# First batch's head: where four projection halves and the next chunk's rows are loaded, how many preparation ticks stand ahead of stage 3, and one half on the short form

## The chip, the cores and the metric

The kernel runs on one core of one Trainium2 chip. The metric is the device time of one execution in microseconds; lower is better. PE is TensorE, DVE is VectorE, ACT is ScalarE, POOL is GpSimd; SP is the engine that only issues transfers. POOL and ACT issue some transfers too.

## The reference

Two blocks in a row. The first mixes along the sequence with a filter in the frequency domain, the second is a SwiGLU feed-forward block on the result:

```python
X = np.fft.rfft(x, axis=1)                      # x: (8, 3008, 256)
Y = X * (filt_r + 1j * filt_i)[None]            # 1505 frequencies
y = np.fft.irfft(Y, n=3008, axis=1)
t = y.reshape(8 * 3008, 256)
g, val = t @ w_gate, t @ w_val                  # (256, 1536) each, float64 in memory
out = (g / (1 + np.exp(-g)) * val) @ w_out      # (1536, 256)
```

The weights arrive as 64-bit floats. The engines compute in 32 bits, so the kernel itself turns each weight into a 32-bit float, out of the two 32-bit words of the 64-bit number.

## The kernel before

**Batches, chunks, groups.** The eight batches are worked through in turn. For each, the transform over 3008 = 47 x 64 is made of matrix products in stages. `stage1` is the transform over 47, `stage2a` that over 64 with the filter, `stage2b` goes back over 64, `stage3` back over 47. `stage3` is done for one chunk of the sequence at a time (four chunks) and leaves the chunk's transposed tokens in `y`. The feed-forward part takes each chunk with three groups of hidden blocks, so a batch has 12 steps. In the first batch the order of the first nine steps is groups outside, chunks 0 to 2 inside, so steps 0, 1 and 2 all use group 0. A step's instructions stand in a list written out by hand (`SCHEDULE`): `P`, `Q`, `A`, `B`, `E` are products on PE (`product`, L1070; profile names `wk`, `wa`, `we`), the lower-case letters evictions on DVE and ACT, `D` and `S` sums on POOL, `W` and `o` the output projection (L1167). Fewer multiplications are bought by sums: `combine_sequence` makes sums of the parts of `y` in `y_t` (mostly on POOL), on which the `A`, `B`, `E` products run.

**The order on an engine is the order in the program.** Every instruction is pinned (`pin`), and each engine takes its own in that order. A transfer's issue stands in the queue of the engine that issues it; most are on SP.

**The head.** Before step 0 the whole spectral part of the first batch has to run, in the scope that opens with `spool0`. `stage2a`, a sum on POOL and `stage2b` are staggered over units `u` of 2 of the 24 frequencies, `stage2b` four units behind. Each `stage2b` (L935) leaves its unit in one of four buffers, and SP stores it to the DRAM tensor `d` (`d2` in the code; L952), from where the rows of a chunk are read back in another order (`load_rows`, L676). The units from 10 on (`N_STORED = 10`) have their share of chunk 0 copied straight into the buffer `f0` (L940); their stores to `d` are put off, and `store_rest(nc.gpsimd)` issues them from POOL. In front of them POOL copies one column of `f0` into `one` (L1276), which holds POOL until chunk 0's rows have landed. Then SP loads chunk 1's rows (`load_t4(1, i)`, two loads of 96 partitions), which need the put-off stores. Seven `idle` products keep PE turning, and `stage3` of chunk 0 follows: four products (`wpd`, L976), each evicted into `y` by ACT (L988, L996) or DVE (L328, L1000).

**The weights.** Between these instructions a `Preparation` converts the weights. They come in halves of 256 KB in a fixed order: 0 to 7 are group 0's hidden weights, 8 to 11 the first four halves of the output projection, 12 on the hidden weights of group 1. `load_weights(i)` (L389) issues a half's load; the first 12 (`N_EARLY`) have places of their own and are loaded by hand-placed calls: 0 to 7 at the start on SP, 8 to 11 from POOL at `u` = 5 to 8. `round_half(i)` is the conversion, spread over ticks: two DVE instructions (L411, L414) with an ACT one (L416), then two DVE ones (L420, L423) for halves below `N_SHORT`, three ACT ones (L427, L429, L431) for the others, then DVE L434 and L438, then POOL (L446 for the projection, with four sums after each second half; L458, L459 for hidden weights). Half `i` < 8 begins at tick 4 `i`; halves 8, 9, 10, 11, 12 begin at ticks 44, 48, 52, 56, 60.

`preparation.tick(step, n)` emits the next `n` ticks where it stands, so its place in the program is the place of those instructions in the engines' queues. `finish(0)` in the head runs to tick 44, the following `tick(0, 5)` to tick 49. In steps 0, 1 and 2 one tick is emitted at each place of the schedule that `tick_at` lists: 18 in step 0, 20 each in steps 1 and 2. Step 3 begins on group 1's weights, in the buffer `lent`, and so needs those.

Of the kernel before, what the change touches and what calls it, by code (L numbers as in the profile page):

```python
# [54 lines left out]
NS, NQ = 24, 64  # L55
NR = 2 * N1
NK = 4 * NS

NH = 4
# [12 lines left out]
N_TWO = NS // NV  # L72
N_QUAD = 8
N_FOUR = NS // 4
N_STORED = 10
# [130 lines left out]
def kernel(  # L206
# [10 lines left out]
    nc = tc.nc  # L217
# [149 lines left out]
    def bits(a):  # L367

        t = wo_t.rearrange("p j i f -> p (j i f)")[:, a:a + 512]
        return t.bitcast(U32).rearrange("p (b f two) -> p b f two", b=2, two=2)  # L370

    def spot_of(i):

        spot = (i - N_EARLY) % 5
        return spot if i < N_LENT and spot < 3 else None

    N_EARLY = 12
    N_SHORT = 9

    def load_weights(i, queue=nc.sync):  # L380
        if i in raws or i >= len(weights):
            return
        if i < N_EARLY:
            raws[i] = early_raw(i)
        elif spot_of(i) is not None:
            raws[i] = bits(4 * 7 * 128 + 512 * spot_of(i))
        else:
            raws[i] = rpool.tile([128, 2, 128, 2], U32, name=f"raw_{i}", tag="raw", bufs=2)
        pin(queue.dma_start(out=raws[i], in_=weights[i][0]))  # L389

    def round_half(i):
# [26 lines left out]
        pf = pw.bitcast(FP32)  # L418
        if i < N_SHORT:
            pin(v.tensor_scalar(out=pf, in0=pw, scalar1=-896.0, scalar2=0.0,  # L420
# [74 lines left out]
    class Preparation:  # L495
# [3 lines left out]
        def __init__(self):  # L499
# [9 lines left out]
            for i, (_, (use, *at)) in enumerate(weights):  # L509
# [14 lines left out]
                def go(half=half, i=i):  # L524
# [3 lines left out]

                times = (0, 1, 2, 3, 4, 6, 7, 9, 10) if i >= N_SHORT else \
                    (0, 1, 2, 3, 4, 6, 9, 10)  # L530
# [33 lines left out]
        def finish(self, step):  # L564
            while any(s <= step and self.at <= t for s, t in self.need.items()):
# [1 line left out]
                self.tick(step)  # L567

    preparation = Preparation()
    tick_at = [set(range(40, 162, 7)), *[{n * 174 // 20 for n in range(20)}] * 2,  # L570
               {0, 6, 12, 18, 24, 31, 37, 42, 72, 78, 84, 90, 96, 102, 108, 114, 122, 130, 138, 146}]

    back_t, quad_t = [], []
# [14 lines left out]
    def bank(name):  # L588
        return wps.tile([128, 512], FP32, name=f"w{name}", tag="w")
# [4 lines left out]
    def idle(t, banks, n):  # L594

        for ps in banks:
            pin(nc.tensor.matmul(out=ps[:, 0:n], lhsT=t[:, 0:128], rhs=t[:, 0:n],
                                 start=True, stop=True))

    class Spectral:  # L600
# [75 lines left out]
            pin(queue.dma_start(out=t.rearrange("p (o n) c -> p o (n c)", o=1),  # L676
                                in_=self.d2_rows[k, steps, :, n].rearrange("s a n c -> s a (n c)")))

        def load_t4(self, k, i):
            t = t4pool.tile([128, NH, C], FP32, name=f"t4_{self.b}_{k}_{i}", tag="t4")  # L680
            at = 2 * k + i
            if self.b == 0:
                self.load_rows(t[0:NK], k, slice(0, NS), ts(i, NH))
            else:

                rows = self.d2_tokens.rearrange("(h n) a c -> h (n a) c", h=2)
                rows = rows[:, ts(at, 2 * NS * NH)]
                for j in range(2):
                    self.load(out=t[64 * j:64 * j + 64, 1],
                              in_=rows[j, 128 * (1 - j):128 * (1 - j) + 64])  # L690
                    self.load(out=t[:, 2 * j], in_=rows[j, 64 * j:64 * j + 128])
            self.t4[k, i] = t
# [498 lines left out]
    spec = Spectral(0)  # L1191

    def run(piece):
        for _ in piece:
            pass

    with tc.tile_pool(name="start", bufs=1) as spool0:
        x0_t = spool0.tile([128, 8, C], FP32, name="x0")
        x0.append(x0_t[0:NR])
        tb0 = spool0.tile([128, NS, 2, 128], FP32, name="tb0")  # L1200
        f0 = spool0.tile([128, NS, C], FP32, name="f0")
        room = spool0.tile([128, 9 * NV, C], FP32, name="room")
        units = [room[:, ts(i, NV)] for i in range(9)] + [x0_t[:, ts(i, NV)] for i in range(4)]
        units += [y_f[:, ts(i, NV * C)].rearrange("p (i c) -> p i c", c=C) for i in range(6)]
        early_places = {"p": (0, 5), "t2": (5, 3), "g": (9, 4), "q": (13, 3), "fr": (16, 3)}
        zero = units[8].rearrange("p i c -> p (i c)")

        one_t = lent[:, 0:2 * NK * 32].rearrange("p (b k) -> p b k", b=2)
        spare = []
        n = 0  # L1210
        while n < NPR - 1:
            pair = ORDER[n][0] in "ABE" and ORDER[n + 1][0] in "ABE"
            spare += [n] if pair else []
            n += 2 if pair else 1

        def early(tag, u):
            first, count = early_places[tag]
            return units[first + u % count]

        def early_raw(i):  # L1220
            if i >= 8:
                return bits(4 * 7 * 128 + 512 * (i - N_EARLY))
            t = wt_t[:, spare[i]:spare[i] + 2].rearrange("p s z f -> p (s z f)")
            return t.bitcast(U32).rearrange("p (b f two) -> p b f two", b=2, two=2)

        unit_t = spool0.tile([128, 128], FP32, name="unit")
        pin(nc.scalar.dma_start(out=unit_t, in_=unit_dram.ap()))
        pin(nc.vector.memset(zero, 0.0))
        pin(nc.scalar.activation(out=one, in_=off_t, func=AF.Silu))
        idle(zero, [bank("idle") for _ in range(3)], 512)  # L1230
        pin(nc.sync.dma_start(out=wf_t, in_=wf_dram.ap()))
        load = [("x", 0), ("w", 0), ("x", 1), ("w", 1), ("w", 2), ("x", 2), ("w", 3), ("w", 4),
                ("x", 3), ("w", 5), ("w", 6), ("w", 7)] + [("t", n) for n in range(6)]
        for what, i in load:
            {"x": spec.load_x, "w": load_weights, "t": spec.load_tables}[what](i)
        for u in range(8):
            idle(zero, [bank("idle") for _ in range(2 * (u in (4, 6)))], 512)
            spec.stage1_first(u)
            preparation.tick(0, (4, 2, 4, 2, 5, 3, 2, 6)[u])
        idle(zero, [bank("idle") for _ in range(2)], 512)  # L1240
        for u in range(2):
            spec.turn(u)
        idle(zero, [bank("idle") for _ in range(2)], 512)
        preparation.tick(0, 5)
        spec.real_part(0)
        lag = 4
        for u in range(N_TWO + lag):
            if u < N_TWO:
                spec.turn(u + 2)
                step = spec.stage2a(u)  # L1250
                next(step)
                if u % 3 == 1:
                    spec.real_part(u + 2)
                next(step)
                preparation.tick(0, 2 * (u < 3), hold=True)
                run(step)
                preparation.release()
                if u % 3 != 2:
                    spec.real_part(u + 1)
            if u == N_TWO + lag - 1:  # L1260
                preparation.finish(0)
            if u >= lag:
                if u == N_TWO:
                    idle(zero, [bank("idle")], 512)
                run(spec.stage2b(u - lag))
            if u == 6:
                pin(nc.sync.dma_start(out=wi_t, in_=wi_dram.ap()))
            if 5 <= u < 9:
                load_weights(u + 3, nc.gpsimd)
            if u == N_TWO - 1:  # L1270
                spec.load_rows(f0[0:56, 0:2 * NH], 0, slice(0, 14), slice(0, 2 * NH), nc.gpsimd)
        spec.load_rows(f0[56:8 * N_STORED, 0:2 * NH], 0, slice(14, 2 * N_STORED), slice(0, 2 * NH),
                       nc.gpsimd)
        for i in range(2):
            spec.t4[0, i] = f0[0:NK, ts(i, NH), :]
        pin(nc.gpsimd.tensor_copy(out=one[0:NK], in_=f0[0:NK, 0, 0:1]))  # L1276
        spec.store_rest(nc.gpsimd)
        for i in range(2):
            spec.load_t4(1, i)
        preparation.tick(0, 5)  # L1280

        idle(zero, [bank("idle") for _ in range(7)], 512)
        for step in (0, 2, 1, 3):
            run(spec.stage3(0, step))
        following = Spectral(1)
        for u in range(2):
            following.load_x(u)
# [26 lines left out]
    def order_of(b):  # L1314

        steps = [divmod(step, NG) for step in range(NCHUNK * NG)]
        if b == 0:
            steps[:NT * NG] = [(k, g) for g in range(NG) for k in range(NT)]
        return steps
# [52 lines left out]
    for b in range(B):  # L1372
        cur, nxt = spec, following if b + 1 < B else None
        spec, following = nxt, Spectral(b + 2)
# [34 lines left out]
        for step in range(NCHUNK * NG + (b == B - 1)):  # L1409
            ghost = step == NCHUNK * NG  # L1410
            k, g = order_of(b)[min(step, NCHUNK * NG - 1)]
# [14 lines left out]
            for place, token in enumerate(SCHEDULE):  # L1426
# [14 lines left out]
                elif op[0] == "t":  # L1441
                    n = int(op[1])
# [20 lines left out]
                if b == 1 and step < 4 and op in FILTER_AT:  # L1463
                    n = FILTER_AT.index(op)
# [49 lines left out]
```

## Time and profile before

| | |
|---|---|
| median of 3 runs | 2822.8 us (2822.79, 2822.8, 2828.36) |
| the profiled execution: its time, its span | 2820.89 us, 2819.0 us |
| PE busy over the span | 99% |
| granted PE clock, mean | 0.998 |
| PE busy in 0 to 80 us | 70.2 us, `idle` products among it |
| PE busy in 80 to 160 us | 74.9 us |
| DMA: share of the 16 engines, 40 to 60 and 60 to 80 us | 0.86, 0.55 |
| first `wpd` of chunk 0, first `wk` of step 0 | 69.63 us, 73.25 us |
| first `wk` of step 3 (on `lent`) | 168.45 us |

Times in the profile are microseconds from the start of the span. A row of a timeline has start, duration (of several merged instructions together), engine, line of the kernel, operation, what is written from what, the shape, the number of instructions, and in brackets how long the engine had been idle and what ended that. SPq is SP's queue of transfer issues; the time in such a row is that of the issue, not of the transfer. A row of waits names who waited for what, the sum in microseconds, the number of times and the longest. PE's ends are modelled, so its starts are the better measure. The medians are of executions without the profiler, the rows are of one profiled execution.

### The profile page before, as it was taken

Reading aid. Unit: us, or ns where it says so; the run is one execution under the profiler, and the core shown is the slowest. Engines: PE = TensorE matmul, PEld = TensorE weight load, DVE = VectorE, ACT = ScalarE, POOL = GpSimd, SP = SyncE. Lnnn points to the kernel's source line nnn. Section 1 sums busy time; section 2 is a strip of 40 time slices with the busy share of each in tenths; the row PEclk is TensorE's granted clock in tenths of the full one; section 3 lists DMA queues with packets and bytes.
Section 4 is the critical chain, followed back from the end, with each engine's and each line's share of the span. In section 5 each row is a group of like instructions: output and inputs, shape, how many; then the busy total and the mean of one; then the engine's idle time right before and its main releaser. Section 6 shows DMA issues by size and latency. Waiting matters only on the chain.

```text
span 2819.0 us, 48524 instructions
## 1 busy us (share of the span) xinstructions
PE 2786.5 (99%) x15446; PEld 2317.1 (82%) x15446; DVE 1995.2 (71%) x4577; ACT 1564.1 (55%) x4179; POOL 1576.7 (56%) x1685
## 2 busy tenths in 40 slices
PE   8999999999999999999999999999999999999998
PEld 6777888888888888888888888878888888888887
DVE  7888767776666766667766677667676767666666
ACT  5775455555555555555555555555554555555554
POOL 4786576465545565456553566445655455545544
PEclk9999999999999999999999999999999999999999
DMA  8687876877666775667666676667765777654543
GB/s 229 227 268 231 291 227 212 287 232 232 179 190 206 248 227 167 208 215 228 221 186 198 209 252 196 190 187 239 226 206 179 214 223 227 192 152 149 153 137 82
DMA packets 362769, 586.59 MB, mean 208 GB/s; under 512 B 198432, under 2 KB 245888, under 8 KB 362340
## 3 DMA queue, kind: packets, MB, share of 16 engines
q1 hardware_dynamic: 337718, 533.52, 60.5%
q10 hardware_dynamic: 22318, 44.38, 5.8%
q0 software_dynamic: 2480, 5.60, 0.7%
q8 instruction: 125, 2.05, 0.3%
q14 instruction: 128, 1.05, 0.1%
HBM read 467.74 MB, written 101.34 MB: 202 GB/s over the span
## 4 chain that ended last, share of the span: by engine, by line
PE 90%; POOL 3%; DVE 2%; DMA 1%; issue 1%; ACT 0%; POOLq 0%; SPq 0%; ACTq 0%; DVEq 0%
PE wa L1070 25%; PE wk L1070 17%; PE wA L1167 16%; PE we L1070 12%; PE wG L1167 8%; PE wF L1167 4%; PE pd L973 3%; PE wqa L711 2%; PE wqc L770 1%; PE wqb L782 1%; POOL h L331 1%; DMA lent<-later_tbl 1%; POOL out_dram L1152 0%; POOL y_t L328 0%; POOL D L331 0%
## 5 line engine op out<-in xcount | busy, mean ns | idle before, releaser
L1070 PE MATMUL wa<-y_t,wt_t 128*128 128x188 f32 x4464 | 879.6, 323 | 2.8 <-ACT m L1105 1.1
L1070 PEld LDWEIGHTS wa<-y_t,wt_t 128*128 128x128 f32 x4464 | 748.0, 190 | 78.0 <-ACT wa L1096 9.3
L1070 PEld LDWEIGHTS wk<-y,wt_t 128*128 128x128 f32 x2976 | 494.6, 190 | 107.1 <-issue 33.9
L1070 PE MATMUL wk<-y,wt_t 128*128 128x188 f32 x2976 | 571.4, 325 | 0.6 <-ACT f L1085 0.6
L331 POOL TENSOR_TENSOR h<-h 128x376 f32<-128x376 f32 x572 | 559.4, 999 | 15.4 <-DVE h L328 15.2
L328 POOL TENSOR_TENSOR h<-h 128x376 f32<-128x376 f32 x190 | 182.9, 983 | 683.0 <-DVE h L1117 683.0
L1167 PE MATMUL wA<-h,wo_t 128*128 128x376 f32 x1532 | 553.2, 483 | 3.9 <-DVE o L328 2.1
L1070 PE MATMUL we<-y_t,wt_t 128*128 128x188 f32 x2232 | 431.8, 323 | 2.0 <-ACT we L1101 1.5
L331 POOL TENSOR_TENSOR D<-f,f 128x376 f32<-128x376 f32 x288 | 279.7, 985 | 257.4 <-ACT f L1085 252.3
L331 DVE TENSOR_TENSOR we<-we,m 128x376 f32<-128x376 f32 x576 | 319.6, 556 | 139.4 <-PE we L1070 72.2
L1070 PEld LDWEIGHTS we<-y_t,wt_t 128*128 128x128 f32 x2232 | 369.2, 190 | 3.6 <-ACT we L1101 2.1
L1167 PEld LDWEIGHTS wA<-h,wo_t 128*128 128x128 f32 x1532 | 275.5, 190 | 114.3 <-issue 7.0
L1105 ACT COPY m<-wa 128x376 f32<-128x376 f32 x576 | 272.6, 473 | 101.6 <-PE wa L1070 98.6
L335 DVE SCALAR_TENSOR_TENSOR y<-wk,c 128x376 f32<-128x376 f32 x480 | 244.4, 540 | 64.3 <-ACT c L1089 37.8
L1112 ACT ACTIVATE g<-wa 128x188 f32<-128x188 f32 x576 | 187.5, 326 | 166.2 <-PE wa L1070 156.5
L1112 ACT ACTIVATE u<-we 128x188 f32<-128x188 f32 x576 | 188.4, 327 | 160.7 <-DVE we L331 153.3
L1167 PE MATMUL wG<-h,wo_t 128*128 128x376 f32 x768 | 274.0, 479 | 0.0
L1089 ACT COPY c<-wk 128x376 f32<-128x376 f32 x288 | 136.4, 474 | 228.7 <-PE wk L1070 198.4
L1101 ACT COPY we<-y 128x376 f32<-128x376 f32 x480 | 222.3, 480 | 19.7 <-DVE h L1117 14.0
L1085 ACT ACTIVATE f<-wk 128x376 f32<-128x376 f32 x288 | 140.3, 487 | 166.6 <-PE wk L1070 115.8
L1117 DVE TENSOR_TENSOR h<-wa,g 128x188 f32<-128x188 f32 x576 | 198.6, 346 | 38.2 <-ACT g L1112 37.9
L1117 DVE TENSOR_TENSOR h<-we,u 128x188 f32<-128x188 f32 x576 | 197.9, 344 | 30.5 <-ACT u L1112 18.9
(190 smaller groups left out, 3515.0 us busy)
## 6 DMA issues: line engine op xcount, KB each, us to landing
wt_t<-w_all SPq DMA_DIRECT2D x174, 896.0 KB
wt_t<-w_all SPq DMA_DIRECT2D x174, 768.0 KB
lent<-filter SPq DMA_DIRECT2D x36, 1024.0 KB
lent<-d SPq DMA_DIRECT2D x84, 256.0 KB
d<-lent ACTq DMA_DIRECT2D x84, 256.0 KB
d<-lent ACTq DMA_DIRECT2D x96, 192.0 KB
lent<-raw SPq DMA_DIRECT2D x144, 128.0 KB
t<-d SPq DMA_DIRECT2D x112, 128.0 KB
```

The costliest lines, as they stand in the source:

```text
L328: return eng.tensor_tensor(out=dst, in0=a, in1=b, op=ALU.add)
L331: return eng.tensor_tensor(out=dst, in0=a, in1=b, op=ALU.subtract)
L335: return nc.vector.scalar_tensor_tensor(out=dst, in0=a, scalar=-1.0, in1=b, op0=ALU.mult, op1=ALU.subtract)
L973: pin(nc.tensor.matmul(out=rows, lhsT=self.t4[k, i][:, j, ts(cb, 128)], rhs=cols, start=j == 0, stop=True, skip_group_check=True))
L1070: pin(nc.tensor.matmul(out=ps[:, z], lhsT=self.wt[:, SLOT[p], z], rhs=rhs, start=start and z == 0, stop=True, skip_group_check=True))
L1085: pin(act.mul(self.small(f"f{i}", f"f{i}", 1), t[f"k{i}"], -1.0))
L1089: pin(act.copy(out=self.small(f"c{i}", f"c{i}", 1), in_=t[f"k{i}"]))
L1101: pin(act.copy(out=self.bank(f"e{at}"), in_=t[f"y{at}"]))
L1105: pin(act.copy(out=self.small(f"m{at}", "m", 4), in_=t[f"a{at}"]))
L1112: pin(act.activation(out=self.small(op, "g", 3, 1)[:, 0], in_=ps[:, 1], func=AF.Silu))
L1117: pin(v.tensor_tensor(out=dst, in0=ps[:, 0], in1=g, op=ALU.mult))
L1167: pin(nc.tensor.matmul(out=self.tiles[at], lhsT=wo_t[:, JB * q + i, WO[p], :], rhs=self.hs[i][:, HID[p]], start=start and i == 0, stop=Tru ...
```

## The change

- Halves 8 to 11 are no longer loaded from POOL at `u` = 5 to 8. Halves 8 and 9 are loaded from SP at `u` = 9, behind the store of unit 5; 10 and 11 from SP behind the loads of chunk 1's rows.
- The first of the two loads of chunk 0's rows from `d` takes 48 partitions instead of 56 and is issued at `u` = 10 instead of 11; the second takes 32 instead of 24.
- Chunk 1's two loads are each cut in two: 80 partitions, whose rows come from stored units, go out from POOL ahead of `store_rest`; the last 16 follow on SP behind it.
- `tick(0, 9)` instead of `tick(0, 5)` ahead of `stage3`, so the head runs to tick 53. Steps 1 and 2 emit 18 ticks each instead of 20.
- `N_SHORT` is 10 instead of 9: half 9 has two DVE instructions in place of three ACT ones.

```diff
-    N_SHORT = 9
+    N_SHORT = 10
...
-    tick_at = [set(range(40, 162, 7)), *[{n * 174 // 20 for n in range(20)}] * 2,
+    tick_at = [set(range(40, 162, 7)), *[{n * 174 // 18 for n in range(18)}] * 2,
...
-        def load_t4(self, k, i):
+        def load_t4(self, k, i, part=None):
+            at = 2 * k + i
+            if part:
+                self.load_rows(self.t4[k, i][8 * N_STORED:NK], k, slice(2 * N_STORED, NS), ts(i, NH))
+                return
             t = t4pool.tile([128, NH, C], FP32, name=f"t4_{self.b}_{k}_{i}", tag="t4")
-            at = 2 * k + i
-            if self.b == 0:
+            if part == 0:
+                self.load_rows(t[0:8 * N_STORED], k, slice(0, 2 * N_STORED), ts(i, NH), nc.gpsimd)
+            elif self.b == 0:
                 self.load_rows(t[0:NK], k, slice(0, NS), ts(i, NH))
...
-            if 5 <= u < 9:
-                load_weights(u + 3, nc.gpsimd)
-            if u == N_TWO - 1:
-                spec.load_rows(f0[0:56, 0:2 * NH], 0, slice(0, 14), slice(0, 2 * NH), nc.gpsimd)
-        spec.load_rows(f0[56:8 * N_STORED, 0:2 * NH], 0, slice(14, 2 * N_STORED), slice(0, 2 * NH),
+            if u == 9:
+                for i in (8, 9):
+                    load_weights(i)
+            if u == 10:
+                spec.load_rows(f0[0:48, 0:2 * NH], 0, slice(0, 12), slice(0, 2 * NH), nc.gpsimd)
+        spec.load_rows(f0[48:8 * N_STORED, 0:2 * NH], 0, slice(12, 2 * N_STORED), slice(0, 2 * NH),
                        nc.gpsimd)
...
         pin(nc.gpsimd.tensor_copy(out=one[0:NK], in_=f0[0:NK, 0, 0:1]))
+        for i in range(2):
+            spec.load_t4(1, i, 0)
         spec.store_rest(nc.gpsimd)
         for i in range(2):
-            spec.load_t4(1, i)
-        preparation.tick(0, 5)
+            spec.load_t4(1, i, 1)
+        for i in (10, 11):
+            load_weights(i)
+        preparation.tick(0, 9)
```

## Prediction

> **What bounds the kernel now.** I read the page first: TensorE (PE) is busy 99% of the span and 90% of the chain that ended last, so the body of the kernel runs at PE's pace. A change in the head pays only where PE stands still, and whatever the head loses or gains is carried to the end, because everything behind it follows in a fixed order.
>
> ```profile
> span 2819.0 us, 48524 instructions
> PE 2786.5 (99%) x15446; PEld 2317.1 (82%) x15446; DVE 1995.2 (71%) x4577; ACT 1564.1 (55%) x4179; POOL 1576.7 (56%) x1685
> ```
>
> Then the timelines of the engines, 40 to 200 us. PE starts chunk 0's inverse (`wpd`) at 69.63 and the first product of the feed-forward part (`wk`) at 73.25. From there to 168.45, where step 3 begins on the weights in `lent`, 95.2 us pass. The same instructions back to back need 80.4 us: 156 products at 0.3185 (49.7), 48 `pd` at 0.216 (10.4), 28 projections at 0.6325 (17.7), 3 `pa` at 0.865 (2.6); the prices are the distances of the starts where nothing waits (four `wa` rows 0.637 apart, eight `pd` 0.865, four `wG` 1.265). So steps 0 to 2 hold 14.8 us of slack, by the same sum 8.0 of it in step 0 and 6.8 in steps 1 and 2. Behind 168 us PE runs without a gap to 215. What can be won is in the head and in those 14.8 us.
>
> How the head ends is read on POOL, then SP, then the vector engines (start, duration, instruction; in brackets the idle time before and who ended it):
>
> ```profile
> 64.47 0.56 POOL L676 DMA_DIRECT2D f<-d  x1
> 69.52 0.18 POOL L1276 COPY one<-f 96x1 f32<-96x1 f32 x1 [4.49 <-DMA f<-d]
> 70.00 1.49 POOL L952 DMA_DIRECT2D d<-x  x2 [0.30 <-issue]
> 74.97 2.28 POOL L328 TENSOR_TENSOR y_t<-y_t 128x376 f32<-128x376 f32 x2 [3.47 <-DVE y_t L328]
> ...
> 80.13 0.97 POOL L331 TENSOR_TENSOR D<-f,f 128x376 f32<-128x376 f32 x1
> ```
>
> POOL waits for the last rows of chunk 0, then issues the two stores that the head had put off, and only then gets `y_t`. SP stands behind those stores:
>
> ```profile
> 74.57 1.67 SPq L676 DMA_DIRECT2D t<-d  x2
> 76.30 1.82 SPq L618 DMA_DIRECT2D x<-in_x_dram  x4
> ```
>
> ```profile
> SPq L676 <- DMA d<-x: 10.1, 2, 9.5
> ```
>
> SP's loads of chunk 1 wait 9.5 us at one stretch, until the second store (issued 70.75) has landed at about 74.55. Everything behind them on SP waits too. In the kernel before nobody needs it at once. VectorE and ScalarE have free time just there:
>
> ```profile
> 68.98 0.28 DVE L414 TENSOR_SCALAR pw<-wo_t 128x256 uint32<-128x256 uint32 x1
> 72.63 0.35 DVE L328 TENSOR_TENSOR y<-wpd,y 128x188 f32<-128x188 f32 x1 [3.36 <-PE wpd L976]
> ```
>
> ```profile
> 70.77 0.48 ACT L988 COPY y<-wpd 128x376 f32<-128x376 f32 x1 [1.19 <-PE wpd L976]
> ```
>
> **What the Trainium skill says.** "TensorE: Matmul & The Clock Gate", Architectural detail: ACT and DVE are strict FIFO. So one preparation instruction whose data are late holds every eviction behind it; the trace agrees (ScalarE's copy at 54.29 waits 3.55 us for a store, and VectorE behind it sits 1.98). The same page, Part 1: an idle window of about 3.4 us halves PE's clock. The trace agrees: after PE's pauses between 78.4 and 81.8 the granted clock is 0.50 in 82 to 84 us and 0.67 in 84 to 86. "DMA: Bandwidth & Descriptors", Two DMAs through the same engine are not ordered: the issuer must wait for the store's completion before it reads the same bytes back; that is the 9.5 us above.
>
> **The change part by part.**
>
> *Four projection halves leave POOL's queue; 8 and 9 go to SP behind the store of unit 5, 10 and 11 behind chunk 1's rows.* POOL loses four issues (0.76, 0.59, 0.55, 0.56), which stood beside its sums. 1 MB no longer mixes with the stores between 48 and 57 us, where the DMA share is 0.8 to 1.06. ScalarE's wait for the store of unit 0 (issued 48.39, reused at 54.29) should shrink: 0.5 MB at the 350 GB/s of 50 to 54 us is 1.5 us at most, and VectorE's gap of 1.98 caps it. Against that, halves 8 and 9 now stand ahead of the stores of units 6 to 9 on SP: two issues of 0.4 fit into SP's 1.4 us of idle before 58.91, but 0.5 MB arrive at 58 to 60, and the second load of chunk 0 carries 256 KB instead of 192. I take the head as 0.6 us sooner at `one` (bounds: 1.4 sooner, 0.5 later).
>
> *Chunk 1's rows split.* 80 of 96 rows go out on POOL between `one` and the put-off stores: two issues at 0.57 (the row of `f<-d`, whose 56 and 24 rows cost the same). The stores thus start 1.14 later, and 640 KB are ahead of them in POOL's queue: 2 us at 320 GB/s, of which I count 0.9 as not hidden (bounds 0 and 2). The second store lands at 74.55 + 1.14 + 0.9 = 76.6 on the old clock. The last 16 rows, on SP, still wait for it: the early load does not remove the wait. Two issues at 0.83 (I assume the price doesn't depend on the rows; lower bound 0.4 as for the small `x` loads) end at 78.3. Chunk 1's first `pd`, which waited 1.25 us for its rows at 79.69, no longer does.
>
> *Halves 10 and 11 behind that, and nine ticks instead of five ahead of stage 3.* This is the part that decides. By the program's order, the four more ticks and half 9's short form put six VectorE instructions in front of chunk 0's first sum (L328 `y<-wpd`): L438 of half 8, L420, L423, L434 of half 9, and **L411 and L414 of half 10**; and L416 of half 10 on ScalarE in front of its first copy (L988). The first four cost 0.42 + 0.28 + 0.28 + 0.43 = 1.4 us and fit the 3.36 idle. But L411 reads half 10, which SP issues only at 78.3. What such a load takes from SP is seen later in the trace, where a product waits for one of 256 KB (SP's row, then PE's):
>
> ```profile
> 316.03 0.39 SPq L618 DMA_DIRECT2D lent<-d  x1
> ```
>
> ```profile
> 319.49 1.10 PE L892 MATMUL pb<-lent 128*128 128x256 f32 x4 [0.44 <-DMA lent<-d]
> ```
>
> That is 3.5 us from issue to reader; the other such one took 4.0, and the first weight of the kernel, under full load, 5.2. So half 10 is there at 81.8, L411 (0.28) and L416 (0.42) follow, and L988 starts at 82.4 instead of 70.77: 11.6 late, less 0.6 from the head: **11.0**.
>
> Queued behind this wait: on VectorE the sums of `y`, on ScalarE the copies of `y`; for these wait POOL's `y_t` sums, D01 and all of PE's products, so PE stands from about 73 to 84. Some is given back at once: before, copy to `y_t` took 4.2 us (70.77 to 74.97), because each eviction waited for its `wpd`; with all four banks full the same chain is some 2.3 us by its own durations. Left at POOL's `y_t`: 11.0 - 1.9 = **9.1**. PE's half clock after the pause costs little: POOL's 5.2 us to D01 cover the first products, and before, PE was slowed in 82 to 86 as well. From D01 on step 0 has the same 18 ticks and nearly the same instructions, one half further on; half 9's three ScalarE steps are gone, chunk 1 has its rows: 0.6 back.
>
> *Steps 1 and 2 at 18 ticks instead of 20.* Four ticks are about one half: six VectorE, four ScalarE and two to five POOL instructions, some 6 us of work on three engines, of which only what stood in PE's gaps counts. Those gaps are 6.8 us, about 4 of them at 154 to 165, behind ScalarE's `m` (1.14) and `we` (1.18). I take 1.5 back (bounds 0 and 4). Both kernels have run 108 ticks by step 3, so nothing differs from there; PE's order is the same throughout.
>
> *The sum:* 9.1 - 0.6 - 1.5 = **7.0 us** slower. The profiled execution took 2820.89 (span 2819.0 and 1.9 around it), 1.9 below the median of 2822.8; so it would become 2827.9, and the median 2829.8.
>
> **The rivals.** *The wait is short (no measurable change).* Half 10 comes early enough to be mostly absorbed: the head gains its full 1.4, the stores land without delay (75.7), SP issues the 16 rows at 0.4 each, and the load takes 3.0, since the DMA queues are nearly empty there (share 0.03 in 68 to 70): L988 at 79.0, 8.2 late, 6.3 at `y_t`; with 4 given back in steps 0 to 2 this is 2.3 slower, 2825. For it: the light DMA load. Against: every load in this trace with a reader waiting took 3.5 or more, and two queues would both have to do better than their rows here.
>
> *Faster: the slack is what the ticks filled.* If preparation on VectorE, ScalarE and POOL makes most of the 14.8 us of slack, the ticks taken from steps 1 and 2, halves 8 and 9 finished before step 0, and POOL's earlier projections free it. It decides when more than 9.1 us come back; at 13 of 14.8 the time is 4 shorter, 2819. For it: VectorE is busy 100% in 100 to 110 and 150 to 160. Against: step 0 keeps its 18 ticks, and half the slack is in it.
>
> *The wait is longer.* The 640 KB cost the stores their full 2 us and half 10 lands after 5 us as under load: 2.6 more, some 2832 to 2834.
>
> **How the numbers follow.** A measurement of this kernel tells about 0.2% (5.6 us) from no change. Slower, the wait as summed (0.57) or longer (0.06): from 5.6 to 11 us. The same, the short wait (0.30): up to 5.6. Faster (0.07). Within the likeliest case the bounds of landing, issue and give-back make about 3 us each way, 2828.5 to 2834. For eight in ten the range reaches down into the short wait, to 2823.5, and up to 2834.5. The time is that of the likeliest, 2829.8.
>
> **What would show it.** In the profile after: L411 on VectorE just ahead of `y<-wpd`, with some 9 us or more of idle ended by a DMA of `wo_t`; `y<-wpd` near 82 instead of 72.6; SP's 16 rows near 76; PE idle from 73, with a granted clock of 0.5 following; step 3's first `wk` on `lent` some 7 us after 168.45; and the same distance from there to the end. I am wrong in the decisive step if `y<-wpd` comes before 76, and in the give-back if the delay at `y_t` and that at step 3 differ by more than 5.

## The result and the profile after

The kernel after takes 2833.16 us in the median (2831.65 to 2837.68, 8 runs), the kernel before 2822.96 (2820.21 to 2828.36, 8 runs): 1.0036 of the time, with a 95% interval of 1.0025 to 1.0047, so 10.2 us slower. The profiled execution took 2832.3 us. The page after, its span and PE's share:

```profile
span 2830.4 us, 48533 instructions
PE 2788.5 (99%) x15446; PEld 2322.5 (82%) x15446; DVE 1995.2 (70%) x4579; ACT 1563.2 (55%) x4176; POOL 1575.2 (56%) x1683
```

The span grew by 11.4 us, PE's busy time by 2.0. So over nine of the eleven microseconds are time in which PE stands. VectorE's and ScalarE's timelines show where (start, duration, instruction, idle time before it):

```profile
83.23 0.29 DVE L411 TENSOR_SCALAR wo_t<-wo_t 128x256 uint32<-128x256 uint32 x1 [14.85 <-DMA wo_t<-in_moe_w_out_dram]
...
84.43 0.35 DVE L328 TENSOR_TENSOR y<-wpd,y 128x188 f32<-128x188 f32 x1 [0.70 <-ACT y L993]
```

```profile
83.61 0.42 ACT L416 ACTIVATE wo_t<-wo_t 128x256 f32<-128x256 uint32 x1 [16.25 <-DVE wo_t L411]
83.94 0.83 ACT L993 COPY y<-wpd 128x376 f32<-128x376 f32 x2
```

The first preparation instruction of half 10 waits 14.85 us for its weights, and right behind it come chunk 0's evictions: the first copy 13.2 us later than before (83.94 for 70.77), the first sum 11.8 later. POOL's and SP's timelines, with the same columns, show why the weights are late:

```profile
61.49 0.62 POOL L945 DMA_DIRECT2D f<-x  x1 [2.73 <-ACT x L940]
65.76 0.57 POOL L676 DMA_DIRECT2D f<-d  x1 [3.65 <-DMA f<-x]
69.71 0.18 POOL L1282 COPY one<-f 96x1 f32<-96x1 f32 x1 [3.38 <-DMA f<-d]
70.24 1.16 POOL L676 DMA_DIRECT2D t<-d  x2 [0.35 <-issue]
71.37 1.50 POOL L957 DMA_DIRECT2D d<-x  x2
...
86.24 2.28 POOL L328 TENSOR_TENSOR y_t<-y_t 128x376 f32<-128x376 f32 x2 [12.61 <-DVE y_t L328]
```

```profile
78.11 1.30 SPq L676 DMA_DIRECT2D t<-d  x2
79.50 0.87 SPq L389 DMA_DIRECT2D wo_t<-in_moe_w_out_dram  x2
```

SP's own waits, and from the list of transfers the put-off stores on POOL (their number, size of each and time from issue to landing):

```profile
SPq L676 <- DMA d<-x: 15.8, 1, 15.8
```

```profile
d<-x POOLq DMA_DIRECT2D x2, 256.0 KB, 6.0
```

SP stands 15.8 us for the second store before it may issue the last 16 rows of chunk 1, and half 10 is behind them. The stores went out 1.4 us later than before, behind the 640 KB of chunk 1's rows, and landed 6.0 us after their issue where before it was 3.8. PE then, and its granted clock in stretches of 4 us (length, PE busy, number of matmuls, clock, DMA share, GB/s):

```profile
69.81 6.49 PE L981 MATMUL wpd<-wi_t,f 96*128 96x94 f32 x32 [3.43 <-issue]
84.83 6.46 PE L1075 MATMUL wk<-y,wt_t 128*128 128x188 f32 x20 [8.54 <-DVE y L328]
...
99.72 1.13 PE L981 MATMUL pd<-wi_t,t 96*128 96x94 f32 x8 [2.02 <-ACT y L1001]
...
101.47 2.71 PE L1075 MATMUL wa<-y_t,wt_t 128*128 128x188 f32 x8
```

```profile
70.00:74.00 4.00, 4.00 (x23) 0.56 0.57 116
78.00:82.00 4.00, 0.00 (x0) 0.50 0.37 118
86.00:90.00 4.00, 4.00 (x14) 0.50 0.08 29
98.00:102.00 4.00, 2.28 (x14) 0.90 0.23 73
102.00:106.00 4.00, 4.00 (x21) 0.67 0.01 2
```

PE pauses twice, 3.43 us ahead of `wpd` (until chunk 0's rows are there) and 8.54 ahead of `wk`, and its clock is halved from about 71 to 91; a third pause of 2.02 is followed by a second slow stretch. Followed along the program, the delay is 0.2 us at `one`, 11.3 at `y_t`, 13.8 at step 1's first `wk` (115.94 for 102.17), 12.6 at step 3's first (181.00 for 168.45) and 11.4 at the end.

One caution for all that follows: a profile shows one execution, and executions of one kernel differ. Behind step 3 every kernel here has the same order of instructions, and yet that stretch takes between 2647.6 and 2652.3 us in the fourteen profiles. In three of them the clock is halved once more in that stretch; in the kernel before it is at 334.5 to 337.9 us, and the delay of the kernel after drops by 1.7 us at that place. Of 153 executions of the kernel before beside the experiments, the 31 with a mean granted clock of 0.999 have a median span of 2817.5 us, the 18 with 0.996 one of 2824.6. So causes are read at places before step 3, and totals from the medians.

### The profile page after: what moved, and what is told of

The parts are those of the page before. It is cut to its first block, busy times and chain, and to the rows that moved or that the text cites. A ratio compares the mean times of both kernels' runs of the same rounds, so it can differ in the third digit from the quotient of the medians.

```text
span 2830.4 us, 48533 instructions
## 1 busy us (share of the span) xinstructions
PE 2788.5 (99%) x15446; PEld 2322.5 (82%) x15446; DVE 1995.2 (70%) x4579; ACT 1563.2 (55%) x4176; POOL 1575.2 (56%) x1683
## 4 chain that ended last, share of the span: by engine, by line
PE 91%; DVE 2%; POOL 2%; DMA 1%; ACT 0%; issue 0%; SPq 0%; POOLq 0%; ACTq 0%; DVEq 0%
PE wa L1075 25%; PE wk L1075 17%; PE wA L1172 17%; PE we L1075 12%; PE wG L1172 8%; PE wF L1172 4%; PE pd L978 3%; PE wqa L716 2%; PE wqc L775 1%; PE wqb L787 1%; POOL h L331 0%; POOL out_dram L1157 0%; DMA lent<-later_tbl 0%; PE pc L932 0%; DMA filter<-lent 0%
```

## The experiments

Each ran beside the kernel before on the same chip. That one had a median of 2821.14 us beside `swap`, `loads_only`, `ticks_only` and `warm`, 2822.43 beside `pool_halves`, `swap_idle`, `swap_no_split` and `ticks_idle`, 2820.70 beside `after_fill` and `ticks_fill`, and 2822.14 beside `ticks_fill2` and `ticks_fill3`; ratios are to these. "D to `wk`" is the time from POOL's first `D` to step 1's first `wk`, a measure of step 0: 22.0 us before, 24.8 after.

### The wait for half 10: `swap`

```diff
+        for i in (10, 11):
+            load_weights(i)
         for i in range(2):
             spec.load_t4(1, i, 1)
-        for i in (10, 11):
-            load_weights(i)
```

> The changed kernel with one order turned round: SP issues halves 10 and 11 ahead of the last 16 rows of chunk 1 instead of behind them. If the wait for half 10 is the cause: half 10 goes out near 62 us, lands by 67, L411 finds it there, the first sum of y (L328) comes back from 84.4 to about 72.5, and the time falls by 8 to 11 us, to 2821 to 2825. If the transfers (split rows, SP halves) are the cause whatever the ticks do: under 3 us of the 10 come back, 2830 to 2833. If the four extra ticks themselves cost: L328 stays 3 us or more late with no idle ended by a transfer, 2828 or more.

Measured: 2826.19 us, ratio 1.0015 (1.0008 to 1.0022), between the ranges of its first two theories. VectorE's and PE's timelines of `swap`:

```profile
77.28 0.35 DVE L328 TENSOR_TENSOR y<-wpd,y 128x188 f32<-128x188 f32 x1 [6.46 <-PE wpd L981]
```

```profile
71.77 7.11 PE L981 MATMUL wpd<-wi_t,f 96*128 96x94 f32 x32 [4.50 <-DMA f<-d]
```

SP still stands 15.3 us for the stores, but half 10 is out at 64.3 and no eviction waits for it. That gives back 5 of the 10 us. The other 5 come earlier: the first sum, at 77.28, is still 4.7 us later than before, with a head that ends 2.1 later (`one` at 71.66) and a `wpd` at half clock (7.1 us for 3.8). The profiled execution is the slowest of the twenty (2829.37 us), so its distances need not be typical.

### The parts alone: `loads_only` and `ticks_only`

`loads_only` is the kernel after with the ticks and the short form of before; `ticks_only` is the reverse, on the kernel before:

```diff
-    N_SHORT = 9
+    N_SHORT = 10
...
-    tick_at = [set(range(40, 162, 7)), *[{n * 174 // 20 for n in range(20)}] * 2,
+    tick_at = [set(range(40, 162, 7)), *[{n * 174 // 18 for n in range(18)}] * 2,
...
-        preparation.tick(0, 5)
+        preparation.tick(0, 9)
```

> All of the changed kernel's loads, but the ticks of the kernel before: five ahead of stage 3, 20 in steps 1 and 2, half 9 on the long form. The wait theory: y is evicted near 72, as before, but L411 of half 10 stands a few instructions further on VectorE and still waits for half 10 to land near 83, so about half of the loss is left: 2826 to 2829. The transfer theory: all of it is left, 2831 to 2834. The tick theory: none is left, 2822 to 2824.

> The kernel before with the ticks alone: nine ahead of stage 3, 18 in steps 1 and 2, half 9 on the short form; all loads where they were, halves 8 to 11 from POOL. The wait theory: halves 10 is there by 61, the six VectorE instructions fit the 3.36 us of idle, y comes at 72.6 to 73, and 1 to 2 us are won in steps 1 and 2: 2820 to 2823. The tick theory: 2828 or more. The transfer theory: about 2823, no change.

Measured: the loads alone 2827.42 us, ratio 1.0022 (1.0013 to 1.0032); the ticks alone 2820.71, ratio 0.9998 (0.9989 to 1.0006), no measurable change. So the ticks cost nothing by themselves that the total shows: the instructions of half 10 ahead of the evictions matter only where half 10 is late. The loads alone cost 6 us. Chunk 0's evictions of `y` don't wait for half 10 here, but in step 0 a shorter form of the same wait is left, in VectorE's timeline:

```profile
88.56 0.47 DVE L411 TENSOR_SCALAR wo_t<-wo_t 128x256 uint32<-128x256 uint32 x1 [2.61 <-DMA wo_t<-in_moe_w_out_dram]
```

PE stands 1.91 us for an eviction behind it. The larger part is the late head again, as in `swap`: the first sum comes at 78.03, 5.4 us later than before, behind a `wpd` at half clock.

### Where those come from: `pool_halves` and `swap_no_split`

`pool_halves` is the kernel after, with the four halves back on POOL; the split of chunk 1's rows, the 48 and 32 rows and the nine ticks stay. `swap_no_split` is `swap` without the split.

```diff
-            if u == 9:
-                for i in (8, 9):
-                    load_weights(i)
+            if 5 <= u < 9:
+                load_weights(u + 3, nc.gpsimd)
...
-        for i in (10, 11):
-            load_weights(i)
```

> The changed kernel with all four halves back on POOL at u = 5 to 8; the split of chunk 1's rows, the 48/32 rows of chunk 0 and the nine ticks stay. After turning the order of SP round, 5 us of loss were left, and the second load of chunk 0's rows stood 3.6 us behind the copy before it. If halves 8 and 9 ahead of the stores of units 6 to 9 on SP cause that: the second load goes out within 1 us of the load before it, the column copy comes by 69.5, and the time is 2821 to 2824. If the 48/32 rows or the split cause it: the 3.6 us stay and the time is 2825 to 2827.

> Halves 10 and 11 ahead of chunk 1's rows on SP, and these rows whole again: two loads of 96 partitions from SP behind the put-off stores, nothing of them on POOL. If the 640 KB on POOL hold the stores up: the second store lands 3.8 to 4.5 us after its issue instead of 6 to 6.5, SP goes on 3 us sooner, and the time falls by 0 to 2 us, to 2824 to 2826. If they don't: the store takes its 6 us all the same, and chunk 1's first pd is later than with the split, 2826 to 2828.

Measured: `pool_halves` 2823.52 us, ratio 1.0003 (0.9996 to 1.001); `swap_no_split` 2826.07, ratio 1.0012 (1.0005 to 1.0019). POOL's timeline of `pool_halves`:

```profile
63.25 0.55 POOL L676 DMA_DIRECT2D f<-d  x1 [0.30 <-issue]
68.37 0.33 POOL L1281 COPY one<-f 96x1 f32<-96x1 f32 x1 [4.57 <-DMA f<-d]
```

With the halves on POOL the second load of chunk 0's rows waits 0.30 us instead of 3.65, and `one` comes at 68.37. The same load waited 2.9 to 3.7 us in all seven kernels with halves 8 and 9 on SP (the profile names `f<-x` in four of them and the stores, `d<-x`, in three), and 0.3 or less in the others, `pool_halves` with its 48 and 32 rows among them. So it is the two halves on SP, ahead of the stores of units 6 to 9, that make chunk 0's rows late, and not the new cut of those rows: `one` comes at 69.3 to 73.8 in those seven and at 68.1 to 69.5 in the others. Between `swap` (+5.1) and `pool_halves` (+1.1) lie 4 us. Their intervals overlap a little, and they differ in halves 10 and 11 too, so 4 us is not the price of halves 8 and 9 alone.

`swap_no_split` shows the other part, in its list of transfers:

```profile
d<-x POOLq DMA_DIRECT2D x2, 256.0 KB, 3.4
```

Without the rows ahead of them the stores land in 3.4 us; in every kernel with the split it was 6.0 to 7.2, in the others 3.1 to 3.8. The total does not tell it: 1.0012 and 1.0015 overlap. But the stores are waited for at a second place besides SP's 16 rows. ScalarE's first `f` of step 0 waits for them too: 0.55 us before, 2.21 in `swap`. In `pool_halves` the second store lands at 76.7 and `f` starts at 76.89 (the profile names a sum on POOL, done at 76.05), and PE stands:

```profile
77.81 2.88 PE L1075 MATMUL wk<-y,wt_t 128*128 128x188 f32 x8 [3.61 <-ACT f L1090]
```

That uses up what its early head had won. So the split stretches the put-off stores, shown, and PE waits for them; the net cost in the total, `pool_halves` against `ticks_only`, which lacks the split and the new cut of chunk 0's rows, is within the intervals.

### PE's clock in the head: `warm`, `swap_idle`, `ticks_idle`

`warm` is the kernel after with 10 `idle` products for 7, and 12 products into a bank of their own behind `stage3`, to keep PE turning. `swap_idle` is `swap` with 12 `idle` products, `ticks_idle` is `ticks_only` with 9.

```diff
-        idle(zero, [bank("idle") for _ in range(7)], 512)
+        idle(zero, [bank("idle") for _ in range(10)], 512)
...
+        ps = bank("warm")
+        for _ in range(12):
+            pin(nc.tensor.matmul(out=ps, lhsT=zero[:, 0:128], rhs=zero, start=True, stop=True))
```

> The changed kernel with PE kept turning through the pause: ten idle products instead of seven ahead of stage 3 and twelve more behind it (about 0.88 us each at full clock, 10.6 us in all, in a pause of 8.5 to 11). The wait for half 10 stays. If PE's half clock is what turned the 11.3 us of delay at POOL's y_t into 13.8 at step 1: granted clock 1.0 from 70 to 91, wk of step 1 some 2 us nearer, 2830 to 2831.5. If the half clock costs nothing: 2833 as it is.

> Halves 10 and 11 ahead of chunk 1's rows on SP, as before, and twelve idle products ahead of stage 3 instead of seven (five more, 4.4 us, in a pause of 4.5). If half the rest of the loss is PE's half clock: wpd takes 3.8 us instead of 6.5 to 7.1, the granted clock is 1.0 from 68 on, y_t comes 2.5 us sooner after the column copy, and the time falls by 2 to 4 us, to 2822 to 2824. If the clock doesn't matter there: 2826 as without them.

> The kernel before with the nine ticks, and nine idle products instead of seven. With the ticks alone PE paused 2.1 us ahead of wpd and the granted clock fell to 0.58 at 70 to 74, so wpd took 5.7 us instead of 3.8. If that ate what the ticks win: wpd 3.8 us, y_t 1.5 to 2 us sooner, 1 to 2 us faster than with the ticks alone, that is 0.05 to 0.1% under the kernel before. If not: equal to the kernel before.

Measured: `warm` 2833.72 us, ratio 1.0048 (1.0035 to 1.0062); `swap_idle` 2824.56, 1.001 (1.0004 to 1.0017); `ticks_idle` 2821.52, 0.9997 (0.9988 to 1.0005). PE's timeline of `warm`:

```profile
70.14 3.78 PE L981 MATMUL wpd<-wi_t,f 96*128 96x94 f32 x32 [1.20 <-issue]
73.75 10.49 PE L1297 MATMUL wwarm<-room 128*128 128x512 f32 x24
86.12 5.13 PE L1075 MATMUL wk<-y,wt_t 128*128 128x188 f32 x20 [1.88 <-DVE y L328]
```

With a shorter pause `wpd` takes 3.78 us instead of 6.49, so its length was PE's clock. It won nothing, since the evictions waited for half 10 anyway (L411 at 84.52). The fill ended 2 us too soon and PE was slow again at `wk`, so `warm` says nothing on the clock in step 0. In `swap_idle` too `wpd` is at full clock (3.71), and the wait for the stores takes its place, on ScalarE:

```profile
81.29 0.86 ACT L1090 ACTIVATE f<-wk 128x376 f32<-128x376 f32 x2 [4.96 <-DMA d<-x]
```

PE stands 4.66 us for it. The confidence interval of `swap_idle` overlaps that of `swap`. In `ticks_idle`, where the stores land in 3.1 us, that wait is absent, `y_t` comes at 73.75, 1.2 sooner than before, and yet the total is unchanged: D to `wk` takes 24.0 us, with PE's clock at 0.62 in 86 to 90.

### PE's clock in step 0: `after_fill`, `ticks_fill`, `ticks_fill2`, `ticks_fill3`

Extra products ahead of `pd` groups of chunk 1, four on the kernel after, three (or twice three) on `ticks_idle`. In the first two kernels they have one more bank of PSUM, which shifts the banks behind it; in the last two they take the bank of the next `wa` group. With either, the output is no longer the reference's, probably because some sums of the first batch's step 0 change (not isolated); these kernels are read for their times and are no versions to use.

```diff
             i, cb = divmod(step, 2)
+            if self.b == 0 and k == 1 and step in FILL:          # FILL = {2: 4}, {2: 3}, or {0: 3, 2: 3}
+                w = wt_t[:, SLOT["Q0"]]
+                keep = bank(f"fill_{step}")
+                for _ in range(FILL[step]):
+                    pin(nc.tensor.matmul(out=keep[:, 0:256], lhsT=w[:, 0],
+                                         rhs=w.rearrange("p z f -> p (z f)"), start=True, stop=True))
```

> The changed kernel, with four extra products (128x256, on the gate weights, into a bank that nothing reads) ahead of the third pd group of chunk 1, where PE paused for 2.02 us in the changed kernel's profile; at some 0.44 us each they fill most of that pause. Theory A, the clock: the second half-clock stretch (0.50 to 0.62 at 100.5 to 105) goes, PE shows 1.0 there, the stretch from D (91.15) to step 1's first wk (115.94, so 24.8 us) shrinks by 1.5 to 2 us to about 23, and the total falls by 1 to 2 us to some 2831.5. Theory B, step 0 is long because of DVE and ACT coming late behind the slow wk, not because of this second stretch: the stretch from D to wk stays within 0.5 us of 24.8 and the total stays at 2833.

> The kernel before with the nine ticks, idle 9 in place of 7, and three extra products of the same kind ahead of chunk 1's third pd group. Without the extra products this kernel showed a half-clock stretch (0.62 at 86 to 90) and 24.0 us from D (78.93) to step 1's first wk. Theory A, the clock: that stretch goes, D to wk falls to 22 to 22.5 us, step 3's first wk on lent comes 1 us sooner than 168.0, the total 0.5 to 1.5 us below 2821.5. Theory B: D to wk stays near 24, and the total is unchanged.

> As ticks_fill, but the three extra products go into the bank that the next wa group takes, and not into a bank of their own, so that no bank changes place. Theory A, the clock: as ticks_fill, 2816 to 2819 us, 0.1 to 0.2% below the kernel before, D to step 1's first wk near 22.2 us, clock 1.0 from 86 on. Theory B, ticks_fill was fast because the extra bank shifted the order of the banks: no change against ticks_idle, ratio 0.9997, D to wk near 24 us.

> ticks_fill2 with three more products ahead of chunk 1's first pd group, where PE paused for 1.46 us on the rows' DMA and then showed 0.50 at 81 to 84.5. Theory A, the clock: that stretch goes too, D to step 1's first wk falls by another 0.5 to 1.2 us, the total 0 to 1 us below ticks_fill2. Theory B, that stretch is hidden beside DVE and ACT, or comes of the clock's own history rather than of this pause: no difference from ticks_fill2, or up to 0.5 us more where the products push the pd back.

PE's timelines of `ticks_idle` and of `ticks_fill2` at the same place:

```profile
86.60 1.69 PE L976 MATMUL pd<-wi_t,t 96*128 96x94 f32 x8 [1.48 <-ACT y L996]
```

```profile
85.78 1.46 PE L970 MATMUL wfill<-wt_t 128*128 128x256 f32 x6
87.97 1.13 PE L989 MATMUL pd<-wi_t,t 96*128 96x94 f32 x8 [0.73 <-ACT y L1009]
```

And PE's clock in `after_fill`, to be held against the last two rows of the kernel after above:

```profile
98.00:102.00 4.00, 3.70 (x23) 1.00 0.37 124
102.00:106.00 4.00, 4.00 (x28) 1.00 0.01 2
```

| | D to `wk` | ratio to before |
|---|---|---|
| after | 24.8 us | 1.0036 (1.0025 to 1.0047) |
| `after_fill` | 22.5 | 1.0035 (1.0023 to 1.0047) |
| `ticks_only` | 22.3 | 0.9998 (0.9989 to 1.0006) |
| `ticks_idle` | 24.0 | 0.9997 (0.9988 to 1.0005) |
| `ticks_fill` | 22.2 | 0.999 (0.9981 to 0.9998) |
| `ticks_fill2` | 22.2 | 0.998 (0.9969 to 0.9991) |
| `ticks_fill3` | 22.2 | 0.998 (0.9974 to 0.9987) |

In the four filled kernels the slow stretch behind the pause is gone and step 0 is 1.8 to 2.3 us shorter, although PE does more. So that stretch made step 0 long. It came of the short pause, but not of its length alone. `ticks_only` has the pause of the kernel after, unfilled, and kept its clock there, with 22.3 us from D to `wk`:

```profile
89.14 1.13 PE L976 MATMUL pd<-wi_t,t 96*128 96x94 f32 x8 [2.02 <-ACT y L996]
```

The traces show what differs. All changes of the clock in a profile lie a whole number of steps of 3.41 us apart, and where this grid lies differs from execution to execution. PE's busy time in such steps, first in the kernel after, then in `ticks_only` (columns as above):

```profile
97.81:101.22 3.41, 1.50 (x12) 1.00 0.18 57
101.22:104.63 3.41, 3.41 (x14) 0.50 0.13 41
```

```profile
84.33:87.74 3.41, 2.10 (x15) 1.00 1.02 390
87.74:91.16 3.42, 2.02 (x15) 1.00 0.85 291
```

In the kernel after the whole pause lies in one step and leaves PE busy for 1.50 us of it; in `ticks_only` a grid line cuts it, and each part leaves over 2.0. Over the fourteen profiles, between 20 and 2790 us, the clock fell 25 times, each time behind a step in which PE was busy for 0 to 1.96 us. At full clock, steps with 1.60 or less were always followed by a fall and steps with 2.01 or more never; between these either happened. An earlier slow stretch is another matter: `ticks_fill` had 0.50 in 82 to 84 and `ticks_fill2` and `ticks_fill3` had none, with the same 22.2 us; the first three products of `ticks_fill3` gain nothing more, as its second theory said.

On the total the two families differ. With the nine ticks alone and the pause filled the kernel is 0.1 to 0.2% faster than before (medians 2816.71, 2817.08 and 2816.82 us, 4 to 5.3 below their kernels before). `ticks_idle` was 0.9 below its own, so filling the pause brings 3.1 to 4.4, of which step 0 shows 1.8 in the profiles. The executions that were not profiled agree in kind: the median of the mean granted clock over all of them is 0.998 in `ticks_idle` and 0.999 in each of the three filled kernels. The rest lies within the intervals, 2 to 3 us each way, and stays open. `after_fill` is 10.15 us slower than before and the kernel after 10.2: 2.3 us shorter in step 0, 1.6 sooner at step 3 (179.4 for 181.0), and nothing of it in the median. Its interval of 6.5 to 13.3 us cannot show 1.6, so that isn't settled. Nor was it tried whether a fill that leaves all the sums alone keeps the 0.2%. No version that computes the whole reference was measurably faster than the kernel before.

## Why the prediction was right, and where its sizes were off

The decisive step was right: the early load of chunk 1's rows leaves SP waiting for the put-off stores, half 10 is queued behind that wait, and the first preparation instruction of half 10 holds chunk 0's evictions. `swap` shows it, by moving halves 10 and 11 alone. The named signs are there: L411 ahead of the first sum with 14.85 us of idle (9 or more expected), the clock at 0.50; SP's 16 rows at 78.1 and the first sum at 84.4 are each some 2 us later than said, and PE stands from 76 and not 73, because `wpd` itself was slow. The sum of 7.0 us was too small, by these terms, measured in one profile of each kernel:

| term | predicted | measured |
|---|---|---|
| head, at `one` | 0.6 sooner | 0.2 later |
| POOL's two issues ahead of the stores | 1.14 | 1.16 |
| second store's landing, longer by | 0.9 | 2.2 |
| SP's two issues of 16 rows | 1.67 | 1.30 |
| half 10, issue to reader | 3.5 | 3.73 |
| first copy of chunk 0, late by | 11.0 | 13.2 |
| given back in the eviction chain | 1.9 | 1.9 |
| step 0 | 0.6 back | 2.5 lost |
| steps 1 and 2 | 1.5 back | 1.2 back |
| sum, at the start of step 3 | 7.0 | 12.6 |

That the median came within 3.4 us of the forecast is in part luck. The sum puts the whole loss down to the wait for half 10. By `swap` the wait alone is worth some 5 of the 10 us; the rest comes of the head and of step 0, which the sum had as gains, and of chunk 0's slow `wpd`, which it did not have.

**The head.** The gain predicted from POOL's lighter queue is there at its start: VectorE's last sum for `stage2b` (`room`) starts 2.4 us sooner (58.50 for 60.87), and ScalarE's wait for the store of unit 0 is gone. It was lost again where the two halves stand ahead of the stores: the second load of chunk 0's rows waits 3.65 us and went out 1.3 us later than before. The prediction counted two issues of 0.4 and 0.5 MB of traffic, and took 0.6 sooner out of bounds that reached to 0.5 later; it did not follow that the row load waits for stores that now land behind that traffic. "DMA: Bandwidth & Descriptors" of the Trainium skill says it under Issuing engines are not separate DMA queues: transfers of all issuing engines run on the same 16 DMA engines and interleave. The runs here agree: moving the halves off POOL's queue did not take them out of the way, it put them where a reader stood, and that reader waited 2.9 to 3.7 us in place of 0.3 or less.

**The stores.** 640 KB ahead of them cost about the upper bound of 2 us, and not the 0.9 taken. The sum also had only one wait for them, that of SP's 16 rows; the other, of ScalarE's first `f`, is hidden behind the wait for half 10 in the kernel after and comes to light in `pool_halves` and `swap_idle`.

**Step 0.** "PE's half clock after the pause costs little" failed. It held for the first `wk`, which POOL's sums cover. It did not hold behind them: PE paused for 2.02 us at chunk 1's third `pd`, and the clock fell to half once more in full work. `after_fill` shows that this second stretch is worth 2.3 us of D to `wk`. The pause itself is not a result of the slow `wk` ahead of it: it is 1.5 to 2.0 us long in all eight unfilled kernels with nine ticks, `ticks_only` among them, and 1.1 and 0.8 in the two with five, before and `loads_only`. So "nearly the same instructions, one half further on" was not near enough; which instruction makes the difference was not tried. "TensorE: Matmul & The Clock Gate", Part 1, speaks of a free-running activity window of about 3.4 us, and of an idle window as what halves the clock. The traces agree on the window (steps of 3.41 us). They do not agree that it must be idle: 1.50 us of work in it were not enough. The prediction's own example shows this too, since in the kernel before PE's pauses of 1.25 and 0.35 us left it busy for 1.87 us of the 3.41 ahead of 81.9.

**Steps 1 and 2.** This term was right. From step 1's first `wk` to step 3's it is 64.8 to 65.1 us in the twelve kernels with 18 ticks and 66.3 in the two with 20.

**The rivals.** The short wait (2.3 us slower) is refuted by 14.85 us of idle; its low prices for landing and load were not met. The faster case needed over 9.1 us given back; the ticks taken out of steps 1 and 2 free 1.2, and `ticks_only` shows nothing of it in the total. The third case, a longer wait, is the nearest: 2832 to 2834 for 2833.2, and its first half, the stores' full 2 us, is what happened.

## What to carry to other kernels

A load that is issued early does nothing for the wait if its last part still needs the late data; what stands behind that part in the same queue gets the whole wait, so independent loads go ahead of it. Before a transfer is moved to a less busy issuer, look for the reader whose data are in flight at the new place. Then look for every reader of what is delayed: a wait that is hidden behind a longer one comes back when that one is removed. And price PE's pauses twice: the pause itself, and the half clock that can follow even pauses of 1.5 to 2 us. Whether it does depends on where a pause falls, so one profile can't settle it; mean clocks and times of many executions can.

## What the runs showed of the hardware that was not expected

- Two stores of 256 KB landed 3.1 to 3.8 us after their issue on POOL, and 6.0 to 7.2 us with 640 KB of loads issued on POOL in the microseconds before.
- The granted clock has two values in these traces, 1.00 and 0.50; figures between are means over a stretch. It changes on a grid of 3.41 us, and it fell behind every step of the grid in which PE was busy for 1.60 us or less, and behind none with 2.01 or more.
- The 32 records of chunk 0's inverse took 3.7 to 3.8 us at full clock and 6.4 to 7.1 us after a pause of 2.9 to 4.5 us. In the kernel after, the clock was still at 1.00 when the work began (69.81) and fell at 70.5; in `swap` it fell at 70.4, ahead of the work (71.77). Both fit the grid.
- In executions of one and the same kernel, time goes with the mean granted clock: for the kernel before a median span of 2817.5 us at 0.999 and of 2824.6 at 0.996.
